# A transform and two expert layers on one core: PReLU from one relu, and the second layer's operands and weights made in smaller portions

## The chip, the cores and the metric

One Trainium2 chip, one of its cores. The metric is the device time of one execution in microseconds (us); the median of three runs is given, and one further execution was profiled. TensorE is PE (its weight loads PEld), VectorE is DVE, ScalarE is ACT, GpSimd is POOL, SyncE is SP, whose queue issues most transfers.

## The reference

```python
def _attn_ref(x):                       # x: 2 x 3008 x 256
    X = np.fft.fft(x, axis=1)
    X = np.fft.fft(X, axis=2)
    return X.real.astype(np.float32)

def _moe_ref(x, w_in, w_out):           # 6016 x 256, 256 x 2048, 2048 x 256
    h = x @ w_in
    g = np.where(h > 0.0, h, 1.0 * (np.exp(np.minimum(h, 0.0)) - 1.0))
    return (g @ w_out).astype(np.float32)

def _moe2_ref(x, w_in, w_out, alpha):
    h = x @ w_in
    g = np.maximum(h, 0.0) + alpha * np.minimum(h, 0.0)
    return (g @ w_out).astype(np.float32)

def reference(x, ...):
    x = _attn_ref(x).reshape(6016, 256)
    x = _moe_ref(x, moe_w_in, moe_w_out)
    return _moe2_ref(x, moe2_w_in, moe2_w_out, moe2_alpha)
```

The weights are drawn in double precision, so the kernel gets them as 64-bit words and converts them itself.

## The kernel before, in words

**Precision.** A product of float32 numbers is made of three passes over rounded parts (`PASSES`): hi x hi, lo x hi, hi x lo. For each operand the `hi` part is a cast on ACT and the `lo` part a subtraction on POOL or DVE (`hi_lo`, `w_split`, `split_hi`/`split_lo`, `hi_2`/`lo_2`).

**Work.** The 6016 tokens lie in six blocks of twice 512, 480 or 484 columns (`BLOCKS`); the two column sets of a block are the two halves t = 0, 1. Layer 1 runs in 96 ticks (`tick`), 16 per block, each for 128 of the 2048 hidden features: 6 matmuls (`gemm1`, L400), DVE adds the DC term and forms both halves (L537 to L539), ACT makes relu(-h) and its exponential (L556, L558 or, from tick 42 on, L563 into PSUM), DVE combines them (L506, L509), ACT and POOL split the result (L516, L522), and three ticks later 12 matmuls (L416) add it to four accumulators. Blocks 0 and 1 are taken in halves (`SEGS`), block 2 is ticks 32 to 47, 3 is 48 to 63, 4 is 64 to 79, 5 is 80 to 95. The result of a block goes to DRAM (`xd`, L442).

Layer 2 runs in 48 pairs (`pair`), eight per block, each for 256 features. Its input product is a two by two block product made with seven products instead of eight: `product` multiplies one of seven combinations of weights (A11, A12, A22, S1 to S4) with one of seven operands made of the block's quarters (b11, b21, b22, t1 to t4), 3 matmuls each (L590), into four PSUM banks a, d, e, b. The copy of `a` to `p1` (L635) has to be made before A12 adds to `a`, the copy of `d` (L638) before S4, the sum L641 before A22. L645 to L656 form the pre-activations h, PReLU follows (L652 to L663: relu(h), relu(-h) and their combination with -alpha), then the 24 matmuls of the pair before (`second`, L416). The first `hi` cast (feature 0) stands at the pair's end, the second one at the next pair's head (L608), the `lo` parts behind them on POOL (L614):

```python
        if p - 1 in pr:
            hi_2(p - 1, 1)
            lo_2(p - 1, 0)
            lo_2(p - 1, 1, nc.vector if end_game else nc.gpsimd)
        ...
            act(out=p1[:, 0:n], in_=a[:, 0:n], func=ACTF.Copy)
```

**Order.** The order on each engine is that of the program: `manual_schedule` adds nothing but waits. Other work is hooked into ticks and pairs by number (`at`, `at2`) at three places, "pre" (head), "mid" and "end". In a pair, "mid" stands behind PReLU's instructions.

- Weights of layer 2 come in eight pieces of 1 MB, (i, 2, c) and (o, 2, c). A piece is converted in two halves: `conv_y` on ACT (L293), then three steps on DVE (`conv_s`: L310, L312, L314), all three in one tick. Five pieces (`KEEP`) are converted in ticks 44 to 71, stored and fetched again in ticks 84 to 95; three (`DIRECT`) are converted in pairs 0 to 5.
- `w_seven` makes the seven weight combinations of an i piece: four sums on DVE (L375 to L378), casts on ACT and `lo` parts on POOL, at the numbers in `FINAL_1` (ticks) and `FINAL_2` (pairs).
- `prep` makes the seven operands of a block of layer 2 in eight steps: a load, then differences on DVE (L476 to L487), casts on ACT (L361), `lo` parts (L362) on POOL for four and on DVE for b21, b22 and t4. For blocks 1 to 5 the load stands six pairs ahead, four steps five to two pairs ahead in "mid", the last three at the end of the pair before the block.

PSUM holds eight banks: four accumulators, two of tag `mm`, two of tag `ee`; the exponentials of layer 1 from tick 42 on use `ee`, and so do d and e. The SBUF pool `big` has seven buffers, the tag `raw` three.

## Time and profile before

| | us |
|---|---|
| median of 3 runs | 1039.83 (1039.21 to 1042.7) |
| the profiled execution | 1039.48 |
| span of its trace | 1037.7 |
| busy: PE, PEld | 973.0, 768.1 |
| busy: DVE, ACT, POOL | 782.7, 748.9, 605.2 |
| PE's share of the chain that ended last | 56% |

All times of the trace count from the span's start. Matmuls are pipelined and their ends are modelled, so the distance between their starts says more than their length. A wait names who ended it. A clock of 1.00 is TensorE's full speed.

### The profile page before, as it was taken

The numbers are of one execution on the slowest core, as the hardware profiler recorded it, in microseconds if no ns is written. First come the engines' busy times: TensorE is split into PE (matmuls) and PEld (weight loads), VectorE is DVE, ScalarE is ACT, GpSimd is POOL, SyncE is SP. The second block draws the span as 40 slices with busy tenths as digits, with TensorE's granted clock in tenths as the row PEclk, the third lists the DMA queues.
The fourth block names the chain that finished last, engine by engine and source line by source line (L and its number), as shares of the span: only waits on it lengthen the run. The fifth ranks groups of instructions, "written<-read, shape, count | busy, mean of one in ns | idle before, by whom it ended". The sixth has DMA issues, their size and how long they took to land.

```text
span 1037.7 us, 12251 instructions
## 1 busy us (share of the span) xinstructions
PE 973.0 (94%) x4206; PEld 768.1 (74%) x4206; DVE 782.7 (75%) x986; ACT 748.9 (72%) x1026; POOL 605.2 (58%) x465
## 2 busy tenths in 40 slices
...
GB/s 310 327 177 127 33 70 82 51 93 41 21 144 104 44 45 6 82 41 102 123 0 1 1 79 1 1 29 51 1 0 79 1 1 80 1 1 41 1 1 41
DMA packets 27110, 63.04 MB, mean 61 GB/s; under 512 B 3044, under 2 KB 12516, under 8 KB 25000
## 3 DMA queue, kind: packets, MB, share of 16 engines
...
q0 software_dynamic: 256, 0.17, 0.1%
...
## 4 chain that ended last, share of the span: by engine, by line
PE 56%; DVE 21%; ACT 14%; issue 5%; DMA 3%; POOL 1%; SPq 0%; DVEq 0%; ACTq 0%; POOLq 0%
PE acc L416 32%; PE eet L590 9%; PE mmt L590 7%; PE mmt L400 4%; ACT hi L608 4%; DVE ht L539 3%; DVE et L506 2%; DVE pt L537 2%; DVE xo L362 2%; DVE sg L312 2%; ACT et L556 1%; PE eet L400 1%; DMA w<-w_in 1%; ACT hi L516 1%; DVE et L509 1%
## 5 line engine op out<-in xcount | busy, mean ns | idle before, releaser
L416 PE MATMUL acc<-hi,wo 128*128 128x512 f32 (+2 forms) x1536 | 471.2, 388 | 5.3 <-ACT hi L516 2.4
L522 POOL TENSOR_TENSOR lo<-et,hi 128x512 fp32r<-128x512 f32 (+2 forms) x192 | 271.7, 1439 | 126.2 <-ACT hi L516 82.7
L416 PEld LDWEIGHTS acc<-hi,wo 128*128 128x128 f32 x1536 | 289.4, 189 | 63.3 <-ACT hi L516 3.3
L614 POOL TENSOR_TENSOR lo<-et,hi 128x512 fp32r<-128x512 f32 (+2 forms) x190 | 248.7, 1340 | 120.9 <-ACT hi L608 101.6
L416 PE MATMUL acc<-lo,wo 128*128 128x512 f32 (+2 forms) x768 | 299.6, 390 | 9.2 <-POOL lo L522 7.9
L416 PEld LDWEIGHTS acc<-lo,wo 128*128 128x128 f32 x768 | 144.7, 189 | 45.4 <-POOL lo L522 15.3
L556 ACT ACTIVATE et<-ht 128x1024 f32<-128x1024 f32 (+3 forms) x97 | 100.1, 1032 | 90.5 <-DVE ht L539 85.6
L663 DVE SCALAR_TENSOR_TENSOR et<-et,nal_sb,ht 128x1024 f32<-128x1024 f32 (+2 forms) x96 | 127.1, 1324 | 47.8 <-ACT ht L660 43.5
L400 PE MATMUL mmt<-zt,wi 128*128 128x512 f32 (+2 forms) x462 | 124.9, 399 | 5.5 <-DVE ht L539 3.7
L641 DVE TENSOR_TENSOR ht<-eet,ht 128x512 f32<-128x512 f32 (+2 forms) x48 | 32.6, 680 | 111.2 <-ACT ht L638 85.5
L400 PEld LDWEIGHTS mmt<-zt,wi 128*128 128x128 f32 x462 | 85.0, 188 | 33.0 <-DVE ht L539 9.7
L590 PE MATMUL mmt<-xo,wa 128*128 128x512 f32 (+2 forms) x288 | 84.0, 400 | 25.6 <-ACT p L635 25.3
L608 ACT ACTIVATE hi<-et 128x1024 fp32r<-128x1024 f32 (+2 forms) x96 | 97.3, 1031 | 10.7 <-PE acc L416 7.0
L516 ACT ACTIVATE hi<-et 128x1024 fp32r<-128x1024 f32 (+3 forms) x97 | 99.1, 1022 | 2.9 <-DVE et L509 2.5
L590 PE MATMUL eet<-xo,wa 128*128 128x512 f32 (+2 forms) x288 | 82.4, 394 | 11.2 <-DVE ht L641 7.0
L590 PEld LDWEIGHTS mmt<-xo,wa 128*128 128x128 f32 x288 | 52.4, 189 | 45.5 <-ACT p L635 36.8
L590 PE MATMUL eet<-xo,sx 128*128 128x512 f32 (+2 forms) x288 | 81.7, 392 | 0.6 <-POOL sx L362 0.6
L590 PEld LDWEIGHTS eet<-xo,wa 128*128 128x128 f32 x288 | 54.2, 190 | 24.8 <-DVE ht L641 9.2
L509 DVE SCALAR_TENSOR_TENSOR et<-et,ht 128x1024 f32<-128x1024 f32 (+2 forms) x43 | 68.7, 1599 | 0.7 <-ACT et L558 0.7
L506 DVE SCALAR_TENSOR_TENSOR et<-eet,ht 128x512 f32<-128x512 f32 (+2 forms) x108 | 67.9, 670 | 0.7 <-ACT eet L563 0.7
L537 DVE SCALAR_TENSOR_TENSOR pt<-zb,an_sb,mmt 128x512 f32<-128x512 f32 (+2 forms) x77 | 56.2, 730 | 12.8 <-PE mmt L400 12.3
L659 ACT ACTIVATE et<-ht 128x1024 f32<-128x1024 f32 (+2 forms) x48 | 50.2, 1046 | 20.5 <-DVE ht L656 20.0
...
## 6 DMA issues: line engine op xcount, KB each, us to landing
w<-w_in SPq DMA_DIRECT2D x8, 1024.0 KB, 16.8
w<-w_out SPq DMA_DIRECT2D x8, 1024.0 KB, 8.6
vt<-ud SPq DMA_DIRECT2D x6, 1024.0 KB, 4.9
...
xs<-xd SPq DMA_DIRECT2D x4, 1024.0 KB
...
```

The lines of the kernel that those rows point to most:

```text
L400: mm(out=p[:, 0:n], lhsT=lhsT, rhs=rhs, start=(i == 0), stop=(i == len(ops) - 1))
L416: mm(out=accs[L, bl][d][t][:, 0:n], lhsT=w[:, a, o, d * 128:(d + 1) * 128], rhs=(hi, lo)[b][:, t, 0:n], start=(f == first and i == 0), sto ...
L506: stt(out=s["e"][:, i, :], in0=s["x"][i], scalar=-1.0, in1=s["h"][:, i, :], op0=ALU.add, op1=ALU.max)
L509: stt(out=s["e"][:, i], in0=s["e"][:, i], scalar=-1.0, in1=s["h"][:, i], op0=ALU.add, op1=ALU.max)
L516: act(out=s["hi"][:, i, 0:s["n"]], in_=s["e"][:, i], func=ACTF.Copy)
L522: nc.gpsimd.tensor_tensor(out=s["lo"][:, i, 0:n], in0=s["e"][:, i, :], in1=s["hi"][:, i, 0:n].bitcast(F32), op=ALU.subtract)
L537: stt(out=pt[:, 0:n], in0=zb[bl][:, 0:n], scalar=an_sb[:, f:f + 1], in1=p[0], op0=ALU.mult, op1=ALU.add)
L556: act(out=s["e"][:, i], in_=s["h"][:, i], func=ACTF.Relu, scale=-1.0)
L590: mm(out=bank[:, 0:n], lhsT=w2(a), rhs=x2[:, b, 0:n], start=(first and m == 0), stop=(last and m == 2), skip_group_check=True)
L608: act(out=s["hi"][f][:, :, 0:n], in_=s["g"][f], func=ACTF.Copy)
L614: eng.tensor_tensor(out=s["lo"][f][:, t, 0:n], in0=s["g"][f][:, t], in1=s["hi"][f][:, t, 0:n].bitcast(F32), op=ALU.subtract)
L663: stt(out=g[f], in0=g[f], scalar=nal_sb[:, 2 * j + f:2 * j + f + 1], in1=hx[f], op0=ALU.mult, op1=ALU.add)
```

## The change

- PReLU is h + (1 - alpha) relu(-h): the relus of h go, and a scaled difference (`stt`) takes h itself, for the first half of feature 0 straight from bank `a` in PSUM. `oma` holds 1 - alpha.
- In a pair the second `hi` cast and its `lo` parts move behind the copies of `a` and `d`, and "mid" moves ahead of PReLU.
- `prep` becomes `load_xs`, `sub` and `cast`, hooked one by one: `AHEAD` for blocks 2 to 5, `FIRST` for block 1 together with the weights of pairs 0 to 7, `PREP_0` for block 0, whose differences are now made by POOL. All `lo` parts of the operands are POOL's, but for three of block 1. In odd blocks b21, b22 and t4 live in `raw` buffers.
- The conversion in ticks takes one step of DVE per tick, between ticks 34 and 72. The weight sums of pieces (i, 2, 0) to (i, 2, 2) are POOL's, in ticks 41 to 74, and in place, so that A11, A12, A22 and S1 are parts of the stored piece and are split with it; those of (i, 2, 3) stay DVE's, in pair 4.
- The last tick makes its exponential in SBUF, so that d and e are free for pair 0.

```diff
 KEEP = [
-    (("i", 2, 0), 42, 44, 47, 84),
-    (("o", 2, 0), 46, 50, 53, 86),
-    (("i", 2, 1), 52, 56, 59, 89),
-    (("o", 2, 1), 58, 62, 65, 93),
-    (("i", 2, 2), 64, 68, 71, 95),
+    (("i", 2, 0), 31, 34, 81),
+    (("o", 2, 0), 39, 42, 84),
+    (("i", 2, 1), 47, 50, 88),
+    (("o", 2, 1), 55, 58, 92),
+    (("i", 2, 2), 63, 66, 95),
 ]
-DIRECT = [
-    (("o", 2, 2), 95, 0, 1),
-    (("i", 2, 3), 0, 2, 3),
-    (("o", 2, 3), 2, 4, 5),
+FINAL_1 = [(84, "i", 0, 0), (86, "i", 0, 1), (88, "o", 0, 0), (90, "o", 0, 1), (92, "i", 1, 0), (94, "i", 1, 1)]
+DIRECT = {("o", 2, 2): 95, ("i", 2, 3): 95, ("o", 2, 3): 0}
+PREP_0 = (64, 67, 70, 73, 76, 79, 82, 85)
+FIRST = [
+    ((("y", "o", 2, 0),), ()),
+    ((("s", "o", 2, 0),), (("y", "o", 2, 1), ("w", "o", 1, 0), ("w", "o", 1, 1))),
+    ((("s", "o", 2, 1), ("x", 1)), (("y", "i", 3, 0), ("w", "i", 2, 0), ("w", "i", 2, 1))),
+    ((("s", "i", 3, 0),), (("y", "i", 3, 1), ("w", "o", 2, 0))),
+    ((("s", "i", 3, 1), ("sub", 1, "t3")), (("y", "o", 3, 0), ("w", "o", 2, 1), ("cast", 1, "t3"))),
+    ((("sums", 3),), (("sx", 3), ("y", "o", 3, 1))),
+    ((("s", "o", 3, 0), ("sub", 1, "t1")), (("w", "i", 3, 0), ("w", "i", 3, 1), ("cast", 1, "t1"))),
+    ((("s", "o", 3, 1),), (("w", "o", 3, 0), ("w", "o", 3, 1), ("cast", 1, "b11"), ("cast", 1, "b21", "v"))),
+    ((("sub", 1, "t2"), ("sub", 1, "t4")), (("cast", 1, "t2"), ("cast", 1, "b22", "v"), ("cast", 1, "t4", "v"))),
 ]
-FINAL_1 = {("i", 2, 0): (86, 88), ("o", 2, 0): (89, 90), ("i", 2, 1): (91, 93)}
-FINAL_2 = {("o", 2, 1): (0, 0), ("i", 2, 2): (0, 1), ("o", 2, 2): (2, 3), ("i", 2, 3): (4, 5), ("o", 2, 3): (6, 6)}
-PREP_0 = (66, 68, 71, 74, 77, 80, 83, 86)
-PREP = (-6, -5, -4, -3, -2)
+AHEAD = [
+    ((("x",),), ()),
+    ((("sub", "t3"),), (("cast", "t3"),)),
+    ((("sub", "t1"),), (("cast", "t1"),)),
+    ((), (("cast", "b11"),)),
+    ((("sub", "t2"),), (("cast", "t2"),)),
+    ((("sub", "t4"),), (("cast", "b21"),)),
+    ((), (("cast", "b22"), ("cast", "t4"))),
+]
...
-    nal_sb = const.tile([128, NFT], F32, name="nal_sb")
+    oma_sb = const.tile([128, NFT], F32, name="oma_sb")
...
-    def w_seven(c, part):
...
-        tt(out=s[:, 0], in0=w[:, 0, 1], in1=w[:, 1, 1], op=ALU.add)
-        tt(out=s[:, 1], in0=s[:, 0], in1=w[:, 0, 0], op=ALU.subtract)
-        tt(out=s[:, 2], in0=w[:, 0, 0], in1=w[:, 0, 1], op=ALU.subtract)
-        tt(out=s[:, 3], in0=w[:, 1, 0], in1=s[:, 1], op=ALU.subtract)
-        hi_lo(wa[c][:, 0, 3], wa[c][:, 1, 3], s[:, 0], nc.gpsimd)
-        for i in range(3):
-            hi_lo(sx[i][:, 0, 2 * c:2 * c + 2], sx[i][:, 1, 2 * c:2 * c + 2], s[:, i + 1], nc.gpsimd)
+    def sums(c, eng, ks=(0, 1, 2, 3)):
+        if 0 in ks:
+            s3[c] = wk.tile([128, 3, 2, 128], F32, tag="raw", name="s3", bufs=3)
+        s = s3[c]
+        ops = [(s[:, 1], w[:, 0, 0], w[:, 0, 1], ALU.subtract), (w[:, 0, 1], w[:, 0, 1], w[:, 1, 1], ALU.add),
+               (s[:, 0], w[:, 0, 1], w[:, 0, 0], ALU.subtract), (s[:, 2], w[:, 1, 0], s[:, 0], ALU.subtract)]
+        for k in ks:
+            o, a, b, op = ops[k]
+            eng.tensor_tensor(out=o, in0=a, in1=b, op=op)
+
+    def split_sx(c, i):
+        if not sx:
+            sx.extend(wp.tile([128, 2, 8, 128], F32R, tag=tag, name="sx") for tag in ("sa", "sb", "sc"))
+        s = s3[c] if i < 2 else s3.pop(c)
+        hi_lo(sx[i][:, 0, 2 * c:2 * c + 2], sx[i][:, 1, 2 * c:2 * c + 2], s[:, i], nc.gpsimd)
...
-    def prep(bl, step):
+    def load_xs(bl):
...
-        if step == 1:
-            t3 = new()
-            tt(out=t3, in0=b22, in1=b12, op=ALU.subtract)
-            done("t3", t3)
...
-            tt(out=t2, in0=b22, in1=b12, op=ALU.subtract)
-            done("t2", t2)
-            tt(out=b12, in0=b21, in1=t2, op=ALU.subtract)
-        elif step == 5:
-            done("b21", b21, nc.vector)
-        elif step == 6:
-            done("b22", b22, nc.vector)
-        else:
-            done("t4", b12, nc.vector)
...
+    def sub(bl, name, eng=nc.vector):
+        b11, b12, b21, b22 = quarters(bl)
+        if name in ("t3", "t2"):
+            tmp[name] = wk.tile([128, 512], F32, tag="s", name="tx", bufs=4)[:, 0:BLOCKS[bl][2]]
+        o, a, b = {"t3": lambda: (tmp["t3"], b22, b12), "t1": lambda: (b12, b12, b11),
+                   "t2": lambda: (tmp["t2"], b22, b12), "t4": lambda: (b12, b21, tmp["t2"])}[name]()
+        eng.tensor_tensor(out=o, in0=a, in1=b, op=ALU.subtract)
+
+    def operand(bl, name):
+
+        i, j = HOME[name]
+        if i > 1 and bl % 2:
+            if name not in xo[bl]:
+                xo[bl][name] = wk.tile([128, 2, 512], F32R, tag="raw", name="xr", bufs=3)
+            return xo[bl][name][:, 0], xo[bl][name][:, 1]
+        if i not in xo[bl]:
+            xo[bl][i] = big.tile([128, 2, 2, 512], F32R, tag="big", name="xo")
+        return xo[bl][i][:, j, 0], xo[bl][i][:, j, 1]
+
+    def cast(bl, name, eng="g"):
+        n = BLOCKS[bl][2]
+        b11, b12, b21, b22 = quarters(bl)
+        v = {"t3": tmp.get("t3"), "t2": tmp.get("t2"), "t1": b12, "t4": b12, "b11": b11, "b21": b21, "b22": b22}[name]
+        hi, lo = operand(bl, name)
+        hi_lo(hi[:, 0:n], lo[:, 0:n], v, nc.vector if eng == "v" else nc.gpsimd)
...
-                if t < E_PSUM:
+                if t < E_PSUM or t == NT - 1:
                     act(out=s["e"][:, i], in_=s["e"][:, i], func=ACTF.Exp, scale=-1.0)
-            if t >= E_PSUM:
+            if E_PSUM <= t < NT - 1:
...
+        if wgt < 4:
+            k, h = ((0, 0), (1, 0), (1, 1), (0, 1))[wgt]
+            w = wi[2, c].rearrange("p a k (j h f) -> p a k j h f", j=2, h=2)[:, :, k, jj, h]
+        else:
+            w = sx[wgt - 4][:, :, j]
...
         if p - 1 in pr:
-            end_game = p == NP
-            hi_2(p - 1, 1)
             lo_2(p - 1, 0)
-            lo_2(p - 1, 1, nc.vector if end_game else nc.gpsimd)
...
             act(out=p1[:, 0:n], in_=a[:, 0:n], func=ACTF.Copy)
...
+            act(out=h1[:, 1], in_=d[:, 0:n], func=ACTF.Copy)
+        if p - 1 in pr:
+            hi_2(p - 1, 1)
+            lo_2(p - 1, 1, nc.vector if p == NP else nc.gpsimd)
+        if p < NP:
...
             product(p, A22, "t4", e, False, True)
-            act(out=hx[0][:, 0], in_=a[:, 0:n], func=ACTF.Relu)
-            act(out=g[0][:, 0], in_=a[:, 0:n], func=ACTF.Relu, scale=-1.0)
-            tt(out=hx[0][:, 1], in0=d[:, 0:n], in1=v[:, 0:n], op=ALU.add)
-            tt(out=hx[1][:, 0], in0=e[:, 0:n], in1=v[:, 0:n], op=ALU.add)
-            tt(out=hx[1][:, 1], in0=hx[1][:, 1], in1=v[:, 0:n], op=ALU.add)
-            act(out=g[0][:, 1], in_=hx[0][:, 1], func=ACTF.Relu, scale=-1.0)
-            act(out=hx[0][:, 1], in_=hx[0][:, 1], func=ACTF.Relu)
-            act(out=g[1], in_=hx[1], func=ACTF.Relu, scale=-1.0)
-            act(out=hx[1], in_=hx[1], func=ACTF.Relu)
-            pr[p] = dict(n=n, g=g, hi=[None, None], lo=[None, None])
-            for f in range(2):
-                stt(out=g[f], in0=g[f], scalar=nal_sb[:, 2 * j + f:2 * j + f + 1], in1=hx[f], op0=ALU.mult, op1=ALU.add)
         for fn in mid:
             fn()
+        if p < NP:
+            h0 = wk.tile([128, 2, 512], F32, tag="h", name="ht")[:, 1, 0:n]
+            g = [wk.tile([128, 2, 512], F32, tag="e", name="et", bufs=3)[:, :, 0:n] for _ in range(2)]
+            act(out=g[0][:, 0], in_=a[:, 0:n], func=ACTF.Relu, scale=-1.0)
+            tt(out=h0, in0=d[:, 0:n], in1=v[:, 0:n], op=ALU.add)
+            act(out=g[0][:, 1], in_=h0, func=ACTF.Relu, scale=-1.0)
+            tt(out=h1[:, 0], in0=e[:, 0:n], in1=v[:, 0:n], op=ALU.add)
+            tt(out=h1[:, 1], in0=h1[:, 1], in1=v[:, 0:n], op=ALU.add)
+            act(out=g[1], in_=h1, func=ACTF.Relu, scale=-1.0)
+            pr[p] = dict(n=n, g=g, hi=[None, None], lo=[None, None])
+            for o, h, f in ((g[0][:, 0], a[:, 0:n], 0), (g[0][:, 1], h0, 0), (g[1], h1, 1)):
+                stt(out=o, in0=o, scalar=oma_sb[:, 2 * j + f:2 * j + f + 1], in1=h, op0=ALU.mult, op1=ALU.add)
...
-        at(18, lambda: act(out=nal_sb, in_=al_sb, func=ACTF.Copy, scale=-1.0))
+        at(18, lambda: act(out=oma_sb, in_=al_sb, func=ACTF.Copy, scale=-1.0, bias=1.0))
-        for key, t_ld, t0, t1, t_get in KEEP:
+        for key, t_ld, t0, t_get in KEEP:
             at(t_ld, load, key)
-            at_conv(t0, [t0] * 3, *key, 0)
-            at_conv(t1, [t1] * 3, *key, 1)
-            at(t1 + 2, keep_w, key)
+            for i, t in enumerate((t0, t0 + 4)):
+                at_conv(t, (t, t + 1, t + 2), *key, i)
+            if key[0] == "i":
+                at(t0 + 7, sums, key[2], nc.gpsimd, (0, 1), where="end")
+                at(t0 + 8, sums, key[2], nc.gpsimd, (2, 3), where="end")
+                for i in range(3):
+                    at(t0 + 9 + i, split_sx, key[2], i, where="end")
+            at(t0 + 9, keep_w, key)
             at(t_get, fetch_w, key)
...
-        for table, off in ((FINAL_1, 0), (FINAL_2, 1000)):
-            for key, ts in table.items():
-                for i, t in enumerate(ts):
-                    if key[0] == "i":
-                        at(off + t, w_seven, key[2], i, where="end")
-                    else:
-                        at_split(off + t, *key, i)
-        for i, t in enumerate(PREP_0):
-            at(t, prep, 0, i, where="mid")
-        for bl in range(1, NBLK):
-            p0 = 1000 + bl * NFT // 2
-            for i, t in enumerate(PREP):
-                at(p0 + t, prep, bl, i, where="mid")
-            for i in (5, 6, 7):
...
+        for t, kind, c, i in FINAL_1:
...
+        for bl in range(2, NBLK):
+            for i, (pre, mid) in enumerate(AHEAD):
+                for where, todo in (("pre", pre), ("mid", mid)):
+                    for what, *args in todo:
+                        at2(bl * NFT // 2 - len(AHEAD) + i, does[what], bl, *args, where=where)
+        at(PREP_0[0], load_xs, 0, where="mid")
+        for i, name in enumerate(("t3", "t1", "b11", "t2", "t4", "b21", "b22")):
+            t = PREP_0[i + 1]
+            if name[0] == "t":
+                at(t, sub, 0, name, nc.gpsimd, where="end")
+            if name != "t4":
+                at(t + 1, cast, 0, name, where="mid")
+        at(PREP_0[7] + 2, cast, 0, "t4", where="mid")
```

## Rows read from the trace of the kernel before

**Rows 1.** The page's first line.

```profile
span 1037.7 us, 12251 instructions
```

**Rows 2.** The chain that ended last, from 700 on: start us, us, what.

```profile
712.35 5.20 PE acc L416 x24
...
722.10 5.20 PE acc L416 x24
...
991.81 5.44 PE acc L416 x24
1002.01 5.44 PE acc L416 x24
```

**Rows 3.** Timeline of DVE at ticks 42 and 95: start us, us, instruction.

```profile
254.48 0.70 DVE L537 SCALAR_TENSOR_TENSOR pt<-zb,an_sb,mmt 128x480 f32<-128x480 f32 x1
...
484.00 0.74 DVE L537 SCALAR_TENSOR_TENSOR pt<-zb,an_sb,mmt 128x512 f32<-128x512 f32 x1
```

**Rows 4.** Timeline of ACT at pairs 1, 8 and 47.

```profile
506.53 0.58 ACT L635 ACTIVATE p<-mmt 128x512 f32<-128x512 f32 x1
...
599.28 0.57 ACT L635 ACTIVATE p<-mmt 128x512 f32<-128x512 f32 x1
...
1018.47 0.58 ACT L635 ACTIVATE p<-mmt 128x512 f32<-128x512 f32 x1
```

**Rows 5.** Busy time by stretch: stretch, length, engines' busy us (instructions), PEclk, DMA, GB/s.

```profile
254.50:354.50 100.00, 98.28 (x443) 81.91 (x441) 95.00 (x146) 78.77 (x108) 63.23 (x50) 1.00 0.20 71
...
506.50:599.30 92.80, 79.46 (x315) 61.77 (x315) 71.67 (x78) 64.40 (x98) 63.22 (x51) 0.94 0.06 21
```

**Rows 6.** Waits in 506.5:599.3, then 599.3:1018.5: us, times, longest.

```profile
PE mmt L590 <- ACT p L635: 10.5, 5, 2.9
...
PE mmt L590 <- ACT p L635: 14.8, 20, 1.4
```

**Rows 7.** Timeline of ACT in an undisturbed pair of the last block.

```profile
994.33 1.06 ACT L660 ACTIVATE ht<-ht 128x1024 f32<-128x1024 f32 x1
995.29 1.04 ACT L608 ACTIVATE hi<-et 128x1024 fp32r<-128x1024 f32 x1
997.11 1.06 ACT L608 ACTIVATE hi<-et 128x1024 fp32r<-128x1024 f32 x1 [0.78 <-PE acc L416]
```

**Rows 8.** Timeline of POOL and DVE in undisturbed pairs.

```profile
986.27 5.19 POOL L614 TENSOR_TENSOR lo<-et,hi 128x512 fp32r<-128x512 f32 x4 [4.71 <-ACT hi L608]
...
992.46 0.68 DVE L656 TENSOR_TENSOR ht<-ht,v 128x512 f32<-128x512 f32 x1
...
993.30 1.28 DVE L663 SCALAR_TENSOR_TENSOR et<-et,nal_sb,ht 128x1024 f32<-128x1024 f32 x1 [0.16 <-ACT ht L658]
```

**Rows 9.** Timeline of DVE, then POOL, in pair 4.

```profile
546.68 0.69 DVE L641 TENSOR_TENSOR ht<-eet,ht 128x512 f32<-128x512 f32 x1 [1.32 <-ACT ht L638]
...
549.28 1.52 DVE L656 TENSOR_TENSOR ht<-ht,v 128x512 f32<-128x512 f32 x1
550.72 2.31 DVE L663 SCALAR_TENSOR_TENSOR et<-et,nal_sb,ht 128x1024 f32<-128x1024 f32 x1
...
548.95 1.30 POOL L614 TENSOR_TENSOR lo<-et,hi 128x512 fp32r<-128x512 f32 x1
550.20 1.75 POOL L614 TENSOR_TENSOR lo<-et,hi 128x512 fp32r<-128x512 f32 x1
```

**Rows 10.** Timeline of DVE in pair 4; a group of 506.5:599.3 (count, busy us, mean ns).

```profile
554.95 0.42 DVE L310 TENSOR_SCALAR sg<-w 128x512 int32<-128x512 int32 x1
555.40 0.69 DVE L312 SCALAR_TENSOR_TENSOR sg<-w,sg 128x512 int32<-128x512 int32 x1
...
L362 POOL TENSOR_TENSOR sx<-s,sx 128x256 fp32r<-128x256 f32 x6 | 4.6, 785 | 0.0
```

**Rows 11.** Timeline of SP at tick 95; DMA issues of 478:500 (count, KB, us to landing).

```profile
481.86 0.38 SPq L280 DMA_DIRECT2D w<-w_out  x1
...
w<-w_out SPq DMA_DIRECT2D x1, 1024.0 KB, 8.8
```

93 lines of the change are left out of this document (40 added, 53 removed).

## The prediction

> **What bounds the kernel now.** I read the waits first, then the chain of work that ended last, the timelines of single pairs, and the sums by stretch. All sums are made against the profiled execution: 1039.48 us, of which the span is 1037.7 [rows 1]; the median of the runs shown is 1039.83, so 0.3 us lie between the two scales and are neglected.
>
> TensorE is the only engine whose work fills the time. In the chain, two weight-out groups (24 matmuls, 5.44 us, 0.2267 each) of undisturbed pairs follow each other by 10.20 us, which is 45 x 0.2267: such a pair has no gap in PE, and nothing taken from another engine can shorten it. With 480 columns it is 9.75, with 484, between the two, about 9.8 [rows 2]. A tick of layer 1 is 18 matmuls, 4.08 us by the same rate (3.90 and 3.92 in the two narrow blocks).
>
> So what can be won is the time above these rates, in three stretches whose ends I take from the first instruction of a tick (L537) and from the copy at the head of a pair (L635) [rows 3, 4]:
> - Ticks 42 to 95: 484.00 - 254.48 = 229.5 us; PE needs 6 x 3.90 + 16 x 3.92 + 31 x 4.08 = 212.6. Lost: 16.9. DVE is busy 95 of 100 us there [rows 5]: a conversion half puts its three steps into one tick, and PE waits for the bank that DVE empties late.
> - Tick 95 to pair 8: 599.28 - 484.00 = 115.3; PE needs 12 + 36 + 21 + 7 x 45 + 3 = 387 matmuls, 87.7. Lost: 27.6, and the clock was granted at 0.94 there [rows 5].
> - Pairs 8 to 47: 1018.47 - 599.28 = 419.2; PE needs 8 x 10.20 + 8 x 9.75 + 8 x 9.8 + 15 x 10.20 = 391. Lost: 28.
>
> What PE waits for in the pairs is above all the copy of L635 [rows 6]. That copy stands in ScalarE's queue behind both `hi` casts, and the second of them behind the whole PReLU: with nothing disturbed, L660 runs to 995.39, the casts at 995.29 and 997.11 [rows 7]. Any portion of other work pushes this chain past the moment when A12 needs the copy, 12 matmuls or 2.72 us into the pair.
>
> **The change, part by part.**
>
> PReLU. ScalarE loses L652, L658 and L660: 1.06 for the last [rows 7] and about 0.6 for each of the others, which are half as wide, 2.3 us a pair. DVE gets three instructions for two, with the same elements. In a pair at 10.20 us that is worth nothing. It shortens the chain: the first cast needs only the stts of feature 0. From L656's end at 993.14 [rows 8] these are two half-width stts, 0.68 as L656 and 0.64 as half of L663, so the cast starts near 994.5 instead of 995.29 and is out of L635's way.
>
> The second cast behind the two copies. L635 then waits for no cast of feature 1. The cast ends some 3.3 us into the pair instead of 1.1, and POOL's two subtractions behind it (5.19 us for four [rows 8]) end by 5.9; PE wants the first of them 4.76 + 14 x 0.2267 = 7.9 us in. Free, with 3 us of cover.
>
> Operands in portions. From block 2 on, four DVE subtractions, seven casts and seven POOL subtractions are spread over the last six pairs of a block, ahead of the PReLU; before, they stood behind it, and three `lo` parts ran on DVE, all in the block's last pair. The load of the block (one DMA) goes one pair earlier on SP's queue, past nothing that is wanted sooner. Odd blocks take three operands into idle weight buffers, so that none waits for the block before: nothing, as long as those buffers are free. I follow one such pair, with 0 at its first matmul. DVE's `sub` now stands ahead of L641: stts of the pair before end near -0.7, a POOL `lo` runs to 0.5, `sub` 0.5 to 1.1, L641 2.35 to 3.05, wanted by A22 at 18 x 0.2267 = 4.08. The cast on ScalarE fills its wait for bank `a`. No PE wait is left. Of the 28 us I keep 0.7 for each of five block changes (estimate: two evacuations of 0.6 and the first cast still stand ahead of L635, which then ends at 2.9 against 2.72, the next copy at 3.5 against 3.40, and L641 follows). Pairs 8 to 47: 391 + 3.5 = 395, a gain of 24. Ends: 28 (nothing kept) and 14 (2 us for each block more, if the sum of the next paragraph spills over).
>
> The limit behind that. L656 takes 0.68 in a quiet pair [rows 8] and 1.52 where POOL's subtraction lies beside it; L663 takes 1.28 and 2.31 [rows 9]. The excess is what was left of POOL's instruction: the two take turns. So the quiet durations of POOL and of the DVE instructions with two inputs in SBUF add up to one sum per pair. Before: 5.19 + 0.68 + 2 x 1.28 = 8.4. After: 5.19 + 0.68 + 0.64 + 1.28 = 7.8, as the stt on bank `a` has one input in PSUM, and L641 with such an input keeps its 0.69 beside POOL [rows 9]. A portion adds 0.69 + 1.30 = 2.0, the last pair 2.6: 9.8 to 10.4 against 10.20. It just fits. The Trainium skill states this as a rule, in "SBUF — State Buffer", section Who interferes with whom: the pair of ports is an exclusive lock, held for a whole instruction, and the loser blocks fully. The rows here agree, 1.52 against 0.68; by it, work moved from DVE to POOL leaves the pool of time it came from only at POOL's dearer price.
>
> Block 0's pairs (weights of layer 2 and operands of block 1 are made there). Prices: a conversion half 0.42 + 0.69 + 0.69 = 1.8, an `sx` part 0.79 [rows 10], a weight's lo part 1.30 like a quarter of POOL's 5.19, a sum, half as wide as L312, 0.35 to 0.42. Sums for pairs 1 to 7: 12.2, 10.9, 12.9, 11.8, 14.2, 14.2, 11.9, together 88.1 (pair 5: 7.8 + 1.8 + `sub` 0.69 + two weight parts and one operand, 3 x 1.30). The same account of before is 7 x 8.4 = 59, five halves 9, weight parts 7.6, two pieces' combinations 11.8, operands 9.4, together 97, and took 599.28 - 506.53 = 92.8 [rows 4], 0.96 of it (successive instructions overlap a little). So 88.1 x 0.96 = 85, a gain of 8. PE alone would give 71.4 (end: a gain of 21); no gain is the other end.
>
> Tick 95 and pair 0. Removed: pair 0's wait for the banks of the last exponential, at most one DVE and one ScalarE instruction of 0.7. Added: ScalarE's first conversion of (o, 2, 2) stands at the end of tick 95, and its load, issued at 481.86, takes 8.8 us [rows 11]; so it lands at 490.7. ScalarE is there one tick after 484.00, at 488.1, waits 2.6, and the cast of tick 94, L635 and with it A12 queue behind it, by some 2 us net of the wait removed. Six ScalarE instructions between the evacuation of layer 1 and pair 1's L635 become one; L635 of pair 1 comes 22 us after tick 95 instead of 22.5. Together -1, from +4 to -4.
>
> Ticks. Ten conversion halves move to ticks 34 to 72, one step a tick. DVE has five instructions of a tick's own, at most L537's 0.70 to 0.74 each [rows 3], some 3.5 us; with a step of 0.6 that is 4.1 and stays near PE's 4.08, where three steps in one tick did not. DVE also loses the sums of two weight pieces and block 0's operands (2 x 4 sums, 4 subtractions, 3 lo parts, about 8 us quiet). POOL takes 12 sums at about 0.8, 9 `sx` parts and 4 subtractions at 1.3: at the fullest (ticks 73 to 78) 2.6 + 1.3 to 1.6 a tick, still under 4.08. I take 8 of the 16.9 as won; ends 0 (POOL's `lo` parts come as late as DVE's banks did) and 13. Ticks 34 to 41 get two halves, 3.6 us of DVE beside stage B: +1, between 0 and 3.6. SP: the stores of kept weights now wait for POOL's sums, and only loads wanted three ticks later stand behind them: nothing.
>
> Sum: -24 - 8 - 1 - 8 + 1 = -40, from 1039.5 to about 999.
>
> **The rivals.**
>
> A, the forecast: 984 to 1011, with 999 the likeliest. Chance 0.62.
>
> B, the turns of POOL and DVE bind: the portions spill over in every block (gain 14), block 0 gains nothing, ticks half. For it: sums of 14.2 in pairs 5 and 6. Against: the pair's own sum falls by 0.6. It gives 1039.5 - 14 - 4 + 1 = 1022; 1011 to 1035. Chance 0.20. This is that rule of the Trainium skill ("SBUF — State Buffer", Who interferes with whom) carried to its end.
>
> C, slower: L641 is starved. `sub` or a conversion stands ahead of it in DVE's queue; if POOL, once started, keeps its turn through all four `lo` parts, L641 ends at -0.7 + 5.19 + 0.69 + 0.69 = 5.9, and A22 waits 1.8 us; with a conversion 2.9. 16 x 1.8 + 7 x 2.9 = 49: 999 + 49 = 1048. It decides from 41 / 23 = 1.8 us per such pair on. Against it: in [rows 9] DVE got its turn between two POOL instructions. Chance 0.07.
>
> D, it does not do what it says: the waits come from the evacuations and the conversions, not from the queue's order, and ticks only shift: within 3 us of 1039.5. The 20 waits for L635 in 39 pairs [rows 6] speak against it. Chance 0.04.
>
> E, all works: ticks 13, block 0 15, blocks 27: 975 to 984. Chance 0.07.
>
> **The numbers.** Faster by over 0.3% (about what a measurement of this kernel can tell): A, B, E, 0.89. Same: D, 0.04. Slower: C, 0.07. The range 980 to 1025 holds A, six tenths of B and half of E, 0.78.
>
> **What would show it.** Right: L635 of successive pairs 10.2 apart at the block changes too; PE's wait for L635 under 5 us after pair 8; no `xo` lo part on the chain; DVE under 92 of 100 in ticks 42 to 66; pair 8 near 105 us after tick 95. Wrong: PE waiting for L641 or `lo` for over 10 us (C, B), POOL without a pause through the last 30 ticks, or pairs of 12 us left (D).

## The result and the profile after

The changed kernel took 986.7 us (median of 4 runs, 985.57 to 987.81) against 1040.89 (4 runs, 1039.21 to 1042.7) of the kernel before beside it: a ratio of 0.9479, 95% interval 0.9456 to 0.9503. The forecast was 999, in 980 to 1025, and faster with a chance of 0.89. The profiled execution took 987.81 us, of which the span is 986.0 (its page's first line; [rows 1] has the one of before).

All times by stage below, here and for the experiments, come from the one profiled execution of each version (pairs 1 to 8, untouched by five of the experiments, took 79.8 us in all five; but the whole of one version varies by up to 6.9 us: c123 took 1022.49 to 1029.35, and the profiled execution is its longest). They are differences of two starts, as in the prediction: the first DVE instruction of ticks 42 and 95 [rows 3] and ScalarE's copy at the head of pairs 1, 8 and 47 [rows 4]. In the changed kernel these lines are L546 and L641 (timelines of DVE and ACT; start us, us, instruction):

```profile
254.60 0.70 DVE L546 SCALAR_TENSOR_TENSOR pt<-zb,an_sb,mmt 128x480 f32<-128x480 f32 x1
...
476.24 0.75 DVE L546 SCALAR_TENSOR_TENSOR pt<-zb,an_sb,mmt 128x512 f32<-128x512 f32 x1 [0.75 <-PE mmt L413]
...
496.83 0.59 ACT L641 ACTIVATE p<-mmt 128x512 f32<-128x512 f32 x1
...
576.60 0.58 ACT L641 ACTIVATE p<-mmt 128x512 f32<-128x512 f32 x1
...
967.11 0.60 ACT L641 ACTIVATE p<-mmt 128x512 f32<-128x512 f32 x1 [2.33 <-PE mmt L602]
```

| us | to tick 42 | ticks 42-95 | to pair 1 | pairs 1-8 | pairs 8-47 | rest | span |
|---|---|---|---|---|---|---|---|
| before | 254.5 | 229.5 | 22.5 | 92.8 | 419.2 | 19.2 | 1037.7 |
| after | 254.6 | 221.6 | 20.6 | 79.8 | 390.5 | 18.9 | 986.0 |
| gain | -0.1 | 7.9 | 1.9 | 13.0 | 28.7 | 0.3 | 51.7 |

More than half of the gain lies in pairs 8 to 47, as forecast. The sums by stretch (columns as in [rows 5]) say what is left:

```profile
254.60:349.90 95.30, 94.79 (x433) 80.82 (x432) 90.62 (x140) 78.41 (x111) 73.58 (x63) 1.00 0.24 77
...
349.90:379.10 29.20, 27.27 (x113) 22.06 (x113) 24.30 (x37) 23.38 (x33) 20.42 (x16) 0.94 0.14 53
...
379.10:447.10 68.00, 65.40 (x287) 53.08 (x286) 53.63 (x85) 54.95 (x76) 55.53 (x47) 1.00 0.16 52
...
496.80:576.60 79.80, 73.38 (x318) 58.90 (x317) 77.04 (x79) 48.94 (x72) 63.65 (x43) 1.00 0.12 40
576.60:967.10 390.50, 390.50 (x1753) 328.57 (x1752) 255.97 (x339) 226.54 (x312) 253.98 (x186) 1.00 0.07 24
```

In the last row PE is busy for 390.50 of 390.50 us: 39 pairs and four block changes without a gap, where [rows 6] had 14.8 us for the copy alone. The chain shows a change from 512 to 480 columns without one (start us, us; [rows 2] for before):

```profile
640.88 5.44 PE acc L429 x24
...
651.08 5.44 PE acc L429 x24
...
661.07 5.49 PE acc L429 x24
...
671.10 5.20 PE acc L429 x24
...
680.85 5.20 PE acc L429 x24
```

The pitch goes from 10.20 over 9.99 and 10.03 to 9.75, the new width's own. What PE still waits for (us, times, longest) lies mainly in ticks 66 to 72 and 72 to 88, and in block 0's pairs 1 to 8:

```profile
PE acc L429 <- POOL lo L531: 1.9, 1, 1.9
...
PE acc L429 <- POOL lo L531: 2.6, 3, 1.2
...
PE eet L602 <- DVE ht L652: 6.4, 5, 1.6
```

### The profile page after: what moved, and what is told of

Same layout as the page of the kernel before. It is cut to its first block, busy times and chain, and to the rows that moved or that the text cites. A ratio compares the mean times of both kernels' runs of the same rounds, so it can differ in the third digit from the quotient of the medians.

```text
span 986.0 us, 12143 instructions
## 1 busy us (share of the span) xinstructions
PE 955.3 (97%) x4206; PEld 770.0 (78%) x4206; DVE 757.0 (77%) x1002; ACT 650.9 (66%) x877; POOL 653.8 (66%) x492
## 3 DMA queue, kind: packets, MB, share of 16 engines
q1 hardware_dynamic: 25632, 61.03, 18.9%
## 4 chain that ended last, share of the span: by engine, by line
PE 73%; DVE 14%; ACT 5%; issue 3%; POOL 3%; DMA 2%; DVEq 0%; ACTq 0%; SPq 0%; POOLq 0%
PE acc L429 40%; PE eet L602 11%; PE mmt L602 8%; PE mmt L413 6%; POOL lo L531 2%; DVE pt L546 2%; DVE ht L548 2%; DVE et L673 2%; DVE et L518 1%; PE eet L182 1%; PE eet L413 1%; ACT et L565 1%; DVE sg L326 1%; ACT hi L525 1%; PE mmt L182 1%
## 5 line engine op out<-in xcount | busy, mean ns | idle before, releaser
L531 POOL TENSOR_TENSOR lo<-et,hi 128x512 fp32r<-128x512 f32 (+2 forms) x192 | 268.8, 1424 | 93.9 <-ACT hi L525 62.3
L413 PE MATMUL mmt<-zt,wi 128*128 128x512 f32 (+2 forms) x462 | 121.1, 395 | 1.8 <-ACT zt L273 0.8
L652 DVE TENSOR_TENSOR ht<-eet,ht 128x512 f32<-128x512 f32 (+2 forms) x48 | 32.6, 679 | 113.9 <-ACT ht L645 113.9
L620 ACT ACTIVATE hi<-et 128x1024 fp32r<-128x1024 f32 (+2 forms) x96 | 99.9, 1040 | 23.6 <-DVE et L673 22.0
L673 DVE SCALAR_TENSOR_TENSOR et<-et,oma_sb,ht 128x512 f32<-128x512 f32 (+2 forms) x96 | 110.4, 1189 | 0.0
L546 DVE SCALAR_TENSOR_TENSOR pt<-zb,an_sb,mmt 128x512 f32<-128x512 f32 (+2 forms) x77 | 56.2, 730 | 29.6 <-PE mmt L413 29.4
L641 ACT ACTIVATE p<-mmt 128x512 f32<-128x512 f32 (+2 forms) x48 | 28.3, 589 | 74.6 <-PE mmt L602 74.6
L602 PE MATMUL eet<-xo,wi 128*128 128x512 f32 (+2 forms) x216 | 60.8, 390 | 7.0 <-DVE ht L652 7.0
L602 PE MATMUL mmt<-xo,wi 128*128 128x512 f32 (+2 forms) x216 | 60.1, 386 | 0.9 <-ACT p L641 0.9
L572 ACT ACTIVATE eet<-et 128x512 f32<-128x512 f32 (+2 forms) x106 | 58.4, 584 | 3.4 <-DVE et L515 1.8
L602 PE MATMUL eet<-xo,sx 128*128 128x512 f32 (+2 forms) x216 | 60.0, 386 | 0.0
```

The lines of the kernel that those rows point to most:

```text
L413: mm(out=p[:, 0:n], lhsT=lhsT, rhs=rhs, start=(i == 0), stop=(i == len(ops) - 1))
L531: nc.gpsimd.tensor_tensor(out=s["lo"][:, i, 0:n], in0=s["e"][:, i, :], in1=s["hi"][:, i, 0:n].bitcast(F32), op=ALU.subtract)
L546: stt(out=pt[:, 0:n], in0=zb[bl][:, 0:n], scalar=an_sb[:, f:f + 1], in1=p[0], op0=ALU.mult, op1=ALU.add)
L602: mm(out=bank[:, 0:n], lhsT=w[:, a], rhs=x2[b][:, 0:n], start=(first and m == 0), stop=(last and m == 2), skip_group_check=True)
L620: act(out=s["hi"][f][:, :, 0:n], in_=s["g"][f], func=ACTF.Copy)
L673: stt(out=o, in0=o, scalar=oma_sb[:, 2 * j + f:2 * j + f + 1], in1=h, op0=ALU.mult, op1=ALU.add)
```

## Experiments

### Which edit in the pairs does it

Three edits could have freed pairs 8 to 47: the second cast behind the two copies (order), the short PReLU, the operands in portions. Each was undone alone, and then with others.

Order undone (e1):

```
         if p - 1 in pr:
+            hi_2(p - 1, 1)
             lo_2(p - 1, 0)
+            lo_2(p - 1, 1, nc.vector if p == NP else nc.gpsimd)
...
-        if p - 1 in pr:
-            hi_2(p - 1, 1)
-            lo_2(p - 1, 1, nc.vector if p == NP else nc.gpsimd)
```

> The changed kernel with one thing undone: the second hi cast of a pair and its lo parts stand again at the next pair's head, ahead of the copies of a and d. Base: pairs 8 to 47 take 390.5 us, pairs 1 to 8 take 79.8. Theory Q (the order of ScalarE's queue is what freed PE): the copy of a waits again for that cast at every portion, pairs 8 to 47 go to 405 to 415, the whole is 15 to 25 us slower. Theory P (the portions' place and the short PReLU free PE, the cast is ready in time even at the head): pairs 8 to 47 stay within 3 us, block 0 loses 2 to 6, the whole 3 to 8 us slower.

PReLU undone (e2; oma_sb holds -alpha again, g still gets its relu of -h):

```
+            act(out=hh[:, 0], in_=a[:, 0:n], func=ACTF.Relu)
...
+            act(out=h0, in_=h0, func=ACTF.Relu)
...
+            act(out=h1, in_=h1, func=ACTF.Relu)
...
-            for o, h, f in ((g[0][:, 0], a[:, 0:n], 0), (g[0][:, 1], h0, 0), (g[1], h1, 1)):
+            for o, h, f in ((g[0], hh, 0), (g[1], h1, 1)):
```

> The changed kernel with the PReLU of before: relu(h) and relu(-h) by ScalarE and two combinations with -alpha by DVE; the order otherwise as changed. Theory Q: the copies no longer stand behind the PReLU, so pairs 8 to 47 stay at 390.5 within 2 us. Theory C (the PReLU's length decides): the first cast comes 1.5 to 2 us later, pairs 8 to 47 lose 10 us or more. Both, by the turns of POOL and DVE: block 0's pairs lose 0.64 each, 4 to 5 us together.

Portions undone (e3; blocks 2 to 5 get the old lumps, behind the PReLU):

```
+OLD = [(-6, "late", "x"), (-5, "late", "sub", "t3"), (-5, "late", "cast", "t3"), (-4, "late", "sub", "t1"), (-4, "late", "cast", "t1"),
+       (-3, "late", "cast", "b11"), (-2, "late", "sub", "t2"), (-2, "late", "cast", "t2"), (-2, "late", "sub", "t4"),
+       (-1, "end", "cast", "b21", "v"), (-1, "end", "cast", "b22", "v"), (-1, "end", "cast", "t4", "v")]
...
-                        at2(bl * NFT // 2 - len(AHEAD) + i, does[what], bl, *args, where=where)
+                at2(bl * NFT // 2 + off, does[what], bl, *args, where=where)
```

> The changed kernel with the operands of blocks 2 to 5 made as before: behind the PReLU, five to two pairs ahead, and the lo parts of b21, b22 and t4 by DVE at the end of the block's last pair. Theory P: each of the four block changes loses 4 us or more, pairs 8 to 47 go to 406 to 415. Theory Q: with the copies ahead of the cast it costs 0 to 2 us a block, at most 398.

None of the three alone cost more than 3.0 us in pairs 8 to 47 (table below), so no theory that gives the gain to one of them holds. The next ones undo them in company, with the diffs above: order and PReLU (c12), order and portions (c13), all three (c123), PReLU and portions (c23).

> Two parts undone together: the second cast ahead of the copies, and the PReLU of before; operands in portions as changed. Undone alone they cost pairs 8 to 47 3.0 and -0.2 us. Theory R (three parts cover for one another: any one of them left keeps PE fed): pairs 8 to 47 at most 398. Theory M (the two parts that shorten ScalarE's chain ahead of the copy matter, the portions do not): 408 to 419. By both, block 0's pairs take 86 to 90.

> Two parts undone together: the second cast ahead of the copies, and the operands of blocks 2 to 5 made as before; the short PReLU stays. Alone they cost pairs 8 to 47 3.0 and 0.4 us. Theory R: at most 398. Theory M (order and PReLU matter): 395 to 402. Theory P2 (order and portions matter, the PReLU does not): 408 to 419.

> All three undone in pairs 8 to 47: order, PReLU and portions as before; ticks and block 0's portions as changed. All theories: pairs 8 to 47 return to 410 to 420 us, the 419.2 of before; the whole 25 to 32 us slower than the changed kernel, plus 7 for block 0. If it stays under 400, none of the three is the cause.

> The changed kernel, with the old PReLU (six relus' worth of ScalarE) and the operands of blocks 2 to 5 in their old few lumps, so that of the three edits in the pairs only the order of the copies (second cast behind the first two copies) is kept. Theory R (each one of the three covers most of the loss, so one kept is nearly enough): pairs 8 to 47 take 393 to 398 us, the whole 995 to 1003. Rival M (what is kept must shorten ScalarE's own work; order moves nothing): pairs 8 to 47 take 405 to 419, the whole 1008 to 1025. Block 0's pairs 1 to 8 in both 86 to 88, as with the old PReLU alone.

| kept of order, PReLU, portions | us, median | ratio to before, 95% | pairs 1-8 | pairs 8-47 |
|---|---|---|---|---|
| all (after) | 986.7 | 0.9456 to 0.9503 | 79.8 | 390.5 |
| PReLU, portions (e1) | 990.39 | 0.9498 to 0.9552 | 80.9 | 393.5 |
| order, portions (e2) | 995.75 | 0.955 to 0.9591 | 86.5 | 390.3 |
| order, PReLU (e3) | 986.31 | 0.9465 to 0.9504 | 79.8 | 390.9 |
| portions (c12) | 1002.12 | 0.9598 to 0.9663 | 90.5 | 395.1 |
| PReLU (c13) | 995.48 | 0.9537 to 0.9595 | 80.7 | 397.9 |
| order (c23) | 1006.23 | 0.9646 to 0.9692 | 86.3 | 400.2 |
| none (c123) | 1026.14 | 0.9828 to 0.9897 | 90.5 | 419.1 |
| before | 1040.89 | | 92.8 | 419.2 |

With none, pairs 8 to 47 are back at 419.1, so the three edits hold the whole gain there. Kept alone, portions win 24.0 of 28.6, PReLU 21.2, order 18.9; two together win 25.6 to all of it. They are three ways to clear the same wait, the copy's; a smaller one, for the addition into h1, goes with the portions. c23 fell between its theories: 400.2, where R gave 393 to 398 and M 405 or more. c12 went to R, and c13's 397.9 lies inside both R and M. So one edit is worth about two thirds of the gain or more, and no single one clears it all. What PE waits for says why (pairs 8 to 47; c12 first, then c13, c23 and c123, one fence each):

```profile
PE mmt L602 <- ACT p L643: 3.6, 6, 2.0
```

```profile
PE eet L605 <- DVE ht L654: 2.9, 4, 0.9
PE mmt L605 <- ACT p L646: 2.5, 6, 0.9
```

```profile
PE eet L605 <- DVE ht L655: 5.6, 4, 1.7
PE mmt L605 <- ACT p L644: 0.3, 2, 0.2
```

```profile
PE mmt L605 <- ACT p L646: 16.0, 20, 2.0
PE eet L605 <- DVE ht L654: 5.7, 4, 1.5
```

(L641 and L652 of the changed kernel, under their numbers in these.) The wait for the copy is there 20 times for 16.0 us with none kept, almost what [rows 6] had. With order kept it is 0.3: the copy stands ahead of the cast, whatever comes late behind it. What remains then is the addition into h1 behind the lumps in DVE's queue, at the four block changes after block 1's; portions remove that. In block 0 it is otherwise: its portions are part of another table and stand in all of these kernels, and there PReLU is worth 6.7 (86.5 against 79.8; 4 to 5 were expected of the turns), order 1.1 (2 to 6 were expected), both together 10.7.

### What the turns of POOL and DVE are worth

In e7, two subtractions that nothing reads are added on POOL in every pair from 9 on, so that only POOL's share grows:

```
+            if 9 <= p < NP:
+                s, n_ = pr[p - 1], pr[p - 1]["n"]
+                for t in range(2):
+                    nc.gpsimd.tensor_tensor(out=dummy[:, 0:n_], in0=s["g"][1][:, t],
+                                            in1=s["hi"][1][:, t, 0:n_].bitcast(F32), op=ALU.subtract)
```

> The changed kernel with two more POOL subtractions of 128x512 per pair from pair 9 on, into a buffer that nobody reads, behind the lo parts of feature 1. POOL's own time rises from 5.2 to 7.8 us a pair, 9.1 with a portion, below PE's 10.20. Theory L (POOL and DVE's instructions with two inputs in SBUF take turns): the sum is 10.4 in a quiet pair and 12.4 in a portion's, times about 0.92; quiet pairs stay at 10.2, portions' pairs take 11 to 12, pairs 8 to 47 go to 405 to 430. Theory I (each engine has its own room): 391 to 394.

Measured: 1003.02 us (0.9619 to 0.9683), pairs 8 to 47 405.6, inside what L gave. The stage counts and not the whole of the profiled execution, since in this execution the part up to tick 42 was 4.3 us longer than in the changed kernel. The sums of that stretch:

```profile
580.80:986.40 405.60, 402.27 (x1753) 324.70 (x1752) 327.33 (x339) 227.50 (x312) 395.12 (x261) 1.00 0.07 23
```

DVE has the same 339 instructions as in the changed kernel and is busy for 327.33 us instead of 255.97; POOL has 75 more and 141 us more, 1.9 each. So POOL's additions also take 71 us as longer DVE instructions. PE loses only 15, because quiet pairs had that room: counted from copy to copy, pairs of 512 columns without a portion stay at 10.2, those with one go to 10.5 to 11.1, and those at a block change to 12.0 to 13.4 (10.45 to 10.9 in the changed kernel, with 9.1 to 9.5 in the next pair; here 9.1 to 9.5 as well).

In e6, the `lo` parts of weights and operands in block 0's pairs go from POOL to DVE, where such a part is shorter:

```
-        nc.gpsimd.tensor_tensor(out=lo, in0=v, in1=hi.bitcast(F32), op=ALU.subtract)
+        eng.tensor_tensor(out=lo, in0=v, in1=hi.bitcast(F32), op=ALU.subtract)
...
-        "w": lambda kind, c, i: w_split(kind, 2, c, i),
+        "w": lambda kind, c, i: w_split(kind, 2, c, i, nc.vector),
...
-    ((("s", "i", 3, 1), ("sub", 1, "t3")), (("y", "o", 3, 0), ("w", "o", 2, 1), ("cast", 1, "t3"))),
+    ((("s", "i", 3, 1), ("sub", 1, "t3")), (("y", "o", 3, 0), ("w", "o", 2, 1), ("cast", 1, "t3", "v"))),
...
```

> The changed kernel with all lo parts of the weights and operands that are made in pairs 0 to 7 (eleven of POOL's) given to DVE. Theory L (in block 0 POOL and the DVE instructions with two inputs in SBUF take turns and fill the time): each saves about 0.65 of the sum, pairs 1 to 8 fall from 79.8 to 72 to 76. Theory D (DVE's own busy time, 77 of 79.8, binds): 11 x 0.68 is added, 85 to 88.

Measured: 989.16 us (0.9492 to 0.9529); pairs 1 to 8 took 83.3, between both theories and nearer D in number. Sums and waits of that stretch:

```profile
494.90:578.20 83.30, 76.71 (x321) 61.67 (x319) 80.61 (x91) 48.19 (x73) 43.93 (x31) 0.96 0.11 38
```

```profile
PE eet L602 <- DVE ht L652: 6.6, 4, 2.2
```

Laid together record by record, the time in which POOL or a DVE instruction with no PSUM input ran falls from 76.6 of 79.8 us to 71.0 of 83.3. So the turns got cheaper by 5.6 and the stretch longer by 3.5. But PE waits no longer than in the changed kernel: it is idle for 83.30 - 76.71 = 6.6 us here and for 79.80 - 73.38 = 6.4 there, both times for L652. The added time lies in PE's busy time (76.71 against 73.38), at a lower granted clock, in two stretches that follow waits of 2.18 and 1.94 us for L652 (sums by stretch):

```profile
509.85:513.45 3.60, 3.60 (x10) 2.83 (x11) 3.60 (x5) 0.63 (x1) 1.71 (x2) 0.59 0.01 2
534.09:537.60 3.51, 3.51 (x9) 2.74 (x10) 3.27 (x5) 1.76 (x4) 2.55 (x4) 0.54 0.00 0
```

In the changed kernel no wait of these pairs is longer than 1.6 and the clock stays at 1.00. The four executions of e6 were granted 0.993 to 0.995 over the span, those of the changed kernel 0.996 to 0.998, so the falls seem to belong to e6; that its longer single waits bring them is not shown. Neither theory's reason is borne out: 5.6 us less of turns saved no waiting (against L), and the added time is the clock's and not DVE's busy time (against D). What PE waits for is one addition in its place in DVE's queue.

### The ticks

In e4 the three sign steps of a conversion stand in one tick again:

```
-                at_conv(t, (t, t + 1, t + 2), *key, i)
+                at_conv(t, (t, t, t), *key, i)
```

> The changed kernel, with the three sign steps of every conversion inside the ticks in one tick again (as before), all else as changed. Ticks 42 to 66 took 100.1 us before and 95.3 after. Theory S (three steps in one tick put 1.7 to 2.2 us of DVE in front of the next tick's pt): ticks 42 to 66 go back to 98 to 100.5 us, and ticks 42 to 95 to 224 to 228; the whole 990 to 994. Rival S0 (the 4.8 us came from elsewhere, such as the later sums or the earlier loads): ticks 42 to 66 at most 96, ticks 42 to 95 within 1.5 of 221.6.

Measured: 996.84 us (0.9561 to 0.9603). Ticks 42 to 66 took 101.2 (before 100.1, after 95.3), somewhat above S's 98 to 100.5; ticks 42 to 95 225.5, inside it. S is right: one step a tick is worth the whole gain of ticks 42 to 66. The whole is longer than S's 990 to 994, because the same edit costs 4.8 us ahead of these ticks too: two conversion halves stand in ticks 34 to 41, and from the first DVE instruction of tick 34 to that of tick 42 it takes 43.5 us (215.74 to 259.23) instead of 38.7 (215.93 to 254.60).

In e5 the twelve sums run on DVE:

```
-                at(t0 + 7, sums, key[2], nc.gpsimd, (0, 1), where="end")
-                at(t0 + 8, sums, key[2], nc.gpsimd, (2, 3), where="end")
+                at(t0 + 7, sums, key[2], nc.vector, (0, 1), where="end")
+                at(t0 + 8, sums, key[2], nc.vector, (2, 3), where="end")
```

> The changed kernel, with the twelve weight sums inside the ticks on DVE instead of POOL. Theory L (POOL's queue is what is late in ticks 66 to 95, so work taken off it helps): ticks 72 to 88 fall from 67.9 to 66.5 us or less, the whole 984 to 986. Rival D (DVE is the fuller engine in a tick, 0.81 busy against 0.74, so GpSimd was the better place): ticks 42 to 66 or 72 to 88 rise by 1 us or more, the whole 988 to 992. Neither: ticks 42 to 95 within 0.8 of 221.6, so the engine of the sums is of no account.

Measured: 989.45 us (0.9487 to 0.953). Ticks 42 to 66 94.1 (-1.2), 72 to 88 71.0 (+3.1), ticks 42 to 95 together 221.9 against 221.6. L fell. The two others both hold by their words, but two things hide the cost. The first two sums stand in tick 41, ahead of the first instruction of tick 42 by which the stretch is measured, so that ticks 34 to 42 took 40.5 instead of 38.7. And in ticks 66 to 72, 1.6 us were saved only because the clock did not fall there (last section). From tick 34 to tick 95 it is 262.4 against 260.3; set against a changed kernel without that fall, the sums on DVE cost 3.7 us. So D holds, with the whole inside its 988 to 992, and POOL is the better place.

Where the new waits of ticks 66 to 88 come from shows around tick 69 (timelines of POOL, ACT and PE in the changed kernel; in brackets the idle time before and who ended it):

```profile
360.05 1.29 POOL L484 TENSOR_TENSOR tx<-xs 128x512 f32<-128x512 f32 x1
362.08 1.82 POOL L376 TENSOR_TENSOR xo<-tx,xo 128x512 fp32r<-128x512 f32 x1 [0.74 <-ACT xo L375]
363.86 3.77 POOL L531 TENSOR_TENSOR lo<-et,hi 128x512 fp32r<-128x512 f32 x3
...
361.37 0.63 ACT L375 ACTIVATE xo<-tx 128x512 fp32r<-128x512 f32 x1 [1.31 <-POOL tx L484]
...
365.19 0.50 PE L429 MATMUL acc<-lo,wo 128*128 128x512 f32 x1 [1.93 <-POOL lo L531]
```

POOL subtracts (L484), ScalarE waits 1.31 for it and casts (L375), POOL waits 0.74 for the cast and makes the operand's `lo` part (L376). Only then come the `lo` parts of the tick's own hidden values (L531), which PE wants. The queue is held by a round trip for an operand that is not needed before the pairs, some 27 ticks later. b1 issues these casts at the end of their tick, behind L531:

```
-                at(t + 1, cast, 0, name, where="mid")
-        at(PREP_0[7] + 2, cast, 0, "t4", where="mid")
+                at(t + 1, cast, 0, name, where="end")
+        at(PREP_0[7] + 2, cast, 0, "t4", where="end")
```

> The changed kernel, with the seven casts of block 0's operands inside the ticks issued at the end of their tick instead of the middle, so that on POOL's queue the lo part of the tick's own hidden values comes before the lo part of the operand (which waits for the cast, which waits for POOL's own subtraction). Theory H (the new stalls of ticks 66 to 88 are this order in the queue): ticks 66 to 72 take 25 to 27.6 us, 72 to 88 at most 66.5, ticks 42 to 95 217 to 219.5; the whole 982 to 985. Rival K (POOL is just full there, whatever the order): ticks 42 to 95 220 to 222.5, the whole 985.5 to 988.

Measured: 980.69 us (5 runs, 980.08 to 981.35), ratio 0.9427, 0.9406 to 0.9448; that is below the changed kernel's whole interval, and the fastest version here. H is right and was too timid: ticks 42 to 95 took 213.7. The same place, and the four stretches of the ticks:

```profile
359.97 1.29 POOL L484 TENSOR_TENSOR tx<-xs 128x512 f32<-128x512 f32 x1
361.22 3.01 POOL L531 TENSOR_TENSOR lo<-et,hi 128x512 fp32r<-128x512 f32 x2
364.19 1.30 POOL L376 TENSOR_TENSOR xo<-tx,xo 128x512 fp32r<-128x512 f32 x1
```

```profile
254.50:349.80 95.30, 94.78 (x433) 80.81 (x432) 90.70 (x140) 78.41 (x111) 73.62 (x63) 1.00 0.24 77
349.80:374.30 24.50, 24.50 (x110) 20.18 (x109) 23.58 (x37) 21.68 (x31) 19.32 (x15) 1.00 0.17 63
374.30:439.60 65.30, 65.30 (x290) 54.06 (x289) 53.63 (x84) 55.94 (x77) 56.52 (x48) 1.00 0.16 56
439.60:468.20 28.60, 28.60 (x128) 23.64 (x127) 22.61 (x35) 24.33 (x33) 24.92 (x20) 1.00 0.09 32
```

The operand's part now starts 2.11 us later and nobody waits for it; PE is busy for 213.18 of 213.70 us, with the same work on every engine. Of the 7.9 us by which ticks 42 to 95 are shorter than in the changed kernel, 1.6 are the fall of the clock in that kernel's profiled execution (last section); against versions without it, which took 220.0, the order is worth 6.3, and by the medians of the whole 6.0.

## Why the prediction was right, and where it was not

The sign, the order of the gains and the mechanism of pairs 8 to 47 were right; the size was 12 us too small, and the accounts of block 0 and of the ticks were not borne out. The two terms of the pairs came out about as rival E had them (27 and 15), the ticks as in the forecast. Term by term, forecast and measured:

- **Pairs 8 to 47**: -24 and -28.7. The 391 us of PE's rate held; the 3.5 us added for the block changes (five were counted, the stretch holds four) were wrong. The step that failed was that the evacuations and the first cast still push the copy past its time. They do push it: at pair 41 it starts 10.9 us behind the copy of pair 40 (895.71), 0.7 more than a pair takes. But it ends there at 907.20, which is 2.23 us into the pair where 2.9 was forecast, and 0.49 us before A12's first matmul; there was no wait for it at all (timelines of ACT and PE):

```profile
904.49 1.28 ACT L447 ACTIVATE ot<-acc 128x512 f32<-128x512 f32 x2 [2.20 <-PE acc L429]
...
906.61 0.59 ACT L641 ACTIVATE p<-mmt 128x512 f32<-128x512 f32 x1
...
907.69 0.84 PE L602 MATMUL mmt<-xr,wi 128*128 128x512 f32 x3
```

  I also gave the order, the PReLU and the portions each a part; the runs show that they overlap, and that one alone leaves 4.6 to 9.7 us, two at most 3.
- **Block 0's pairs 1 to 8**: -8 and -13.0, the largest mis-sized term, and its account failed twice. First in the counts. With the quiet prices of the prediction and the instructions as the two traces count them, before should have been 41 x 1.30 + 10 x 0.79 on POOL and 7 x 0.68 + 14 x 1.28 + 5 x 1.8 + 8 x 0.39 + 6 x 0.69 on DVE, 100 instead of 97, and after 40 x 1.30 + 3 x 0.79 and 7 x (0.68 + 0.64 + 1.28) + 4 x 1.8 + 4 x 0.39 + 7 x 0.69, 86 instead of 88.1. The prediction's own rule, 86 x 92.8 / 100, then gives 80, which is what was measured. But that is luck, for the account fails in the versions between. Laid together, POOL and DVE occupy 89.4 of 92.8 us before, 81.6 of 90.5 in c123, 80.6 of 86.5 in e2, 76.6 of 79.8 after and 71.0 of 83.3 in e6: from before to c123 the turns fall by 7.8 for 2.3 us of time, from c123 to the changed kernel by 5.0 for 10.7, and in e6 by 5.6 while the time rises.

  What the traces show in its place are two gains of like size ([rows 5], and the row of 496.80 above). PE was idle for 92.80 - 79.46 = 13.3 us before and for 6.4 after; and nearly the same number of matmuls kept it busy for 79.46 us before and 73.38 after, at a granted clock of 0.94 before and 1.00 after. The prediction read that 0.94 and gave it no term. Three stretches of before, behind waits of 2.87, of 2.20, and of 2.31, 0.43 and 0.62 us, hold 4.8 of these 6.1 us, 3.6 x (0.41 + 0.46 + 0.47):

```profile
522.20:525.80 3.60, 3.60 (x10) 2.83 (x11) 1.98 (x3) 1.95 (x4) 3.60 (x4) 0.59 0.00 0
560.50:564.10 3.60, 3.60 (x11) 2.82 (x10) 2.96 (x5) 1.97 (x5) 3.60 (x4) 0.54 0.00 0
573.80:577.40 3.60, 3.58 (x9) 2.83 (x10) 1.38 (x2) 1.06 (x3) 3.60 (x4) 0.53 0.00 0
```

  The idle time of before is mostly the copy's [rows 6]. In c123, with block 0's new tables but the old order and PReLU, it is the addition into h1 instead:

```profile
PE eet L605 <- DVE ht L654: 11.5, 6, 2.8
```

  The short PReLU cuts this most, from 11.0 in e2 to 6.4. In pair 4 of e2, DVE stood 1.14 us for a relu of h by ScalarE that the changed kernel does not have, with four sums and that addition behind it; the other pairs were not followed.
- **Rival C's mechanism** exists there, smaller than priced: PE waits 5 times for L652, 1.6 us at most, where C had 2.9 in every such pair. With the old PReLU it does reach C's price: 3.0 at most in e2, 2.8 in c123. The timelines of DVE and POOL in pair 5 show it:

```profile
539.80 1.66 DVE L326 SCALAR_TENSOR_TENSOR sg<-w,sg 128x512 int32<-128x512 int32 x1
541.49 1.68 DVE L328 SCALAR_TENSOR_TENSOR w<-w,sg 128x512 int32<-128x512 int32 x1
543.09 1.76 DVE L484 TENSOR_TENSOR xs<-xs 128x512 f32<-128x512 f32 x1
544.78 0.68 DVE L652 TENSOR_TENSOR ht<-eet,ht 128x512 f32<-128x512 f32 x1
...
539.52 3.10 POOL L626 TENSOR_TENSOR lo<-et,hi 128x512 fp32r<-128x512 f32 x2 [1.84 <-ACT hi L620]
542.88 3.11 POOL L626 TENSOR_TENSOR lo<-et,hi 128x512 fp32r<-128x512 f32 x2 [0.27 <-ACT hi L620]
```

  Three DVE instructions of the size that takes 0.69 when quiet [rows 10] take 1.66 to 1.76 beside POOL, and L652, with an input in PSUM, keeps its 0.68 behind them. DVE got its turn after each POOL instruction, as [rows 9] had it, so C's price of a whole string of POOL's never came.
- **Ticks 42 to 95**: -8 and -7.9, right by two errors. DVE's steps gave 4.8 in ticks 42 to 66, though DVE stayed at 90.62 of 95.30 (95%; the prediction wanted under 92): spreading mattered, not the sum. "Still under 4.08" was the wrong step on POOL: its sum is under a tick's time, but a queue in this order is late all the same, and b1 shows that this cost 221.6 - 213.7 = 7.9 with the clock's 1.6, about as much as the ticks had won. In versions where the clock did not fall the term is -9.5 (220.0).
- **Tick 95 to pair 1**: -1 and -1.9. The 2.6 us for (o, 2, 2) did not come. Its load was issued 0.7 before the tick's first instruction and landed in 5.5 us, not in 8.8 [rows 11], so about at 481.05, and ScalarE waited 0.46, which the trace puts down to POOL's L531, ended at the same time (queue of SP, timeline of ACT, DMA issues of the stretch):

```profile
475.55 0.38 SPq L294 DMA_DIRECT2D w<-w_out  x1
...
481.09 0.68 ACT L307 ACTIVATE w<-w 128x512 f32<-128x512 f32 x1 [0.46 <-POOL lo L531]
```

```profile
w<-w_out SPq DMA_DIRECT2D x1, 1024.0 KB, 5.5
```

- **Ticks 34 to 41**: +1 and +0.1 (254.48 to 254.60); by e4 it would have been 4.8 more with three steps in one tick.
- **The signs named**: PE did not wait for the copy after pair 8. The copies are not 10.2 apart at the block changes (10.45 to 10.9, then 9.1 to 9.5), PE's work is. DVE's share was missed, and pair 8 came 100.4 us after tick 95, not 105. PE waited 7.0 us for L652 and 9.5 for the `lo` parts of L531 in the whole span, over the 10 that stood for C or B when added, but none of it in pairs 8 to 47.

Rival B was not the outcome, but e7 shows that its limit is near: with 2.6 us more of POOL a pair it is there. What e6 would give with the addition moved ahead in DVE's queue was not tried, so block 0's last 8 us above PE's 71.4, of which 6.4 are waits for L652, stay open.
